# A fused gated-linear-attention and soft-mixture kernel on one core: the first head pair's gating work dealt out anew between three engines, and a fifth identity product ahead of its state product

## The chip, the cores and the metric

One core of one Trainium2 chip runs the whole program. The metric is the device time of one launch in microseconds (us), the median of several runs; lower is better. The engines named below are TensorE (PE, with its weight loads as PEld), VectorE (DVE), ScalarE (ACT), GpSimd (POOL) and SyncE (SP, which issues the DMAs). They run side by side, each through its own instructions in order, and wait for each other through semaphores.

## The reference, cut to what matters

There are 4 x 8 = 32 heads of 768 tokens with 48 channels each, all float32.

```python
f = 1.0 / (1.0 + np.exp(-f_logit))
for t in range(S):
    state = f[:, :, t, :, None] * state + np.einsum('bhd,bhe->bhde', k[:, :, t], v[:, :, t])
    y[:, :, t] = np.einsum('bhd,bhde->bhe', q[:, :, t], state)
x = y.transpose(0, 2, 1, 3).reshape(B * S, H * D)        # 3072 x 384
logits = x @ phi                                         # 32 slots, 4 for each of 8 experts
slot_input = softmax(logits, axis=0).T @ x               # dispatch
slot_out[e] = np.maximum(slot_input[e] @ w1[e], 0.0) @ w2[e]
return softmax(logits, axis=1) @ slot_out                # combine
```

## The kernel before, in words

Two heads lie together on 112 of the 128 partitions (48, a gap of 16, 48) and are called a pair. There are 16 pairs, four to a batch. The tokens of a pair are cut into 6 chunks of 128. For each pair, with the name that the plan gives each step:

- **Gates.** `e` (L325, ACT) is exp(-f), `ln` (L329, ACT) is ln(1 + that), `L` (L333, DVE) sums it along each chunk with a scan, `g` (L336) and `p` (L339, both ACT) are exp(L) and exp(-L), `dk` multiplies k by g and `dq` multiplies q by p, in place (both L342, through the helper `times`; on DVE or POOL). `pend` and `pbx` (POOL, a line of `copy`, L316, for `pbx`) take the last column of each chunk of p.
- **Products on PE.** `kt` (L362) transposes the gated k into PSUM, `kte` copies it out into `kta` (L316). `sc` (L374) makes the scores of three chunks at a time, `mask` (L379, DVE) takes them out under a triangular mask. `kv` (L408) makes each chunk's state from `kta` and v; the scan at L412 (DVE, `sb`) runs the state over the chunks. `ia` (L399) and `ie` (L422) add masked scores times v and q times state into `y`, and `ye` (ACT, L316) copies it out.
- **Mixture.** Logits (L454), transposes of y (L433), running maxima, exponentials and the slot inputs follow one and two pairs behind. After the last pair come the experts' two layers (`up` L620, `down` L666) and the combining products and stores (L712, L721).

The tail's output columns are made in two parts, columns 0 to 255 and 256 to 383 (`PARTS`, `WIDE`), and the order of its steps is written out in `ENDING`.

**What sets the order.** Each step is an `op` with a due number, an engine and the buffers that it reads and writes. A planner (`Plan.run`) holds all steps of the attention stage on a given engine in the order of their due numbers; only the DMAs on SP and the steps of the tail are placed by its estimates. Pair 0 and a few steps of pairs 1 and 2 have their due numbers in the table `START`. Pair 0's gates are done in two halves of 384 columns (called half a and half b below); all other pairs are done whole, in 768 columns. For each `gates` call a pair `es` chooses the engines: `es[0]` for `dk`, `es[1]` for `dq`, where 0 and 1 are POOL and 2 is DVE. Whether `kte` and `pbx` of pair 0 go to DVE or ACT is written at the `op`.

The step `warm` (L313) runs on PE while the first loads come in: products of the 128 x 128 identity with itself, repeated to 512 columns. Nothing reads them. Four are made before the first `kt`.

DMAs share one queue on SP and are issued in order. Weight loads (`lw1`, `lw2`) are put between the loads of q, k, f and v, and each weight load waits for a step of the computation that the planner picks, so that it isn't issued early. With three buffers for f, k and q and two for `L`, `g` and `p`, a load waits until its buffer's last reader has run.

Of the kernel before, what the change touches and what calls it, by code (L numbers as in the profile page):

```python
# [14 lines left out]
B, H, S, D = 4, 8, 768, 48  # L15
# [6 lines left out]
NP = B * H // 2  # L22
# [47 lines left out]
class Plan:  # L70
# [22 lines left out]
    def op(self, name, engs, fn, *args, r=(), w=(), x=(), due=0.0, take=(), free=(), kb=0, home=False, ni=0):  # L93

        name, mode = name if isinstance(name, tuple) else (name, None)
        deps = set()
        for key in r:
            if key in self.writer:
                deps.add(self.writer[key])
        for key in (*w, *x):  # L100
            if key in self.writer:
                deps.add(self.writer[key])
            deps.update(self.readers.get(key, ()))
        fixed = self.fixed and "SP" not in engs
# [100 lines left out]
T = 7.0  # L205
N_F, N_L, N_G, N_P, N_K, N_Q, N_V, N_SC, N_KT, N_S, N_Y = 3, 2, 2, 2, 3, 3, 4, 2, 2, 2, 3
NW1 = 7
N_WARM = 4


@with_exitstack
def gla_soft_moe_kernel(ctx: ExitStack, tc: tile.TileContext, q, k, f, v, vt, phi, w1, w2, out):
# [38 lines left out]
    pbx = [P([128, D, NM], f"pbx{i}") for i in range(N_S)]  # L251
# [19 lines left out]
    mask = P([128, C], "mask")  # L271
# [34 lines left out]
                e = 2 * qq + j  # L306
                nc.gpsimd.memset(emask[:, j, qq, 4 * e : 4 * e + 4], 1.0)

    def warm_up(o):

        u = unit(("warm",))
        for n in range(N_WARM):
            nc.tensor.matmul(u[:, :512], ident, ident.unsqueeze(1).broadcast_to([128, 4, 128]), start=True, stop=True)  # L313

    def copy(o, dst, src):
# [408 lines left out]
    op = plan.op  # L724

    def either(act, dve):
        return {"ACT": act, "DVE": dve}

    op(("warm", "square"), {"PE": 1.75 * N_WARM}, lambda o: warm_up(o), due=-50, take=[(("warm",), "a")], free=[("warm",)], ni=4 * N_WARM)
    op("consts", {"DVE": 0.5}, lambda o: consts(), w=["same"], due=30)  # L730
    op("consts_2", {"POOL": 1.0}, lambda o: consts_2(), w=["emask"], due=40)

    HALVES = (slice(0, S // 2), slice(S // 2, S))

    START = dict(
        e=(-60, -59), ln=(-58, -57), g=(-55, -52), p=(-54, -51),
        L=(-60, -59), dk=(-58, -60), dq=(-57, -55.8), mask=(-54, -53),
        kt=(-9, -7), sc=(-8, -6),
    )
    START["e", 1], START["ln", 1], START["e", 2], START["g", 1], START["p", 1], START["ln", 2] = -56, -53, -50, -49, -48, -47  # L740
    START["L", 1], START["kte", 0], START["scan", 0], START["L", 2] = -56, -55, -52, -51
    START["ye", 0], START["g", 2], START["p", 2] = -46, -45, -44
    START["pbx", 0], START["dk", 1], START["dq", 1], START["pend", 0] = -55.5, -56, -55, -54
# [4 lines left out]
    def attention(i):  # L748

        z = i * T  # L750
        F_, L_, G, PB, K, Q = (
            [(name, i % n, h) for h in range(2)]
            for name, n in (("fb", N_F), ("Lb", N_L), ("gb", N_G), ("pb", N_P), ("kb", N_K), ("qb", N_Q))
        )
        V, Y = ("vb", i % N_V), ("yT", i % N_Y)
        KT, PX, SB = ("ktb", i % N_KT), ("pbx", i % N_S), ("sb", i % N_S)
        SC = [("scb", i % N_SC, h) for h in range(2)]
        b, p = divmod(i, PPB)
# [25 lines left out]
        usual = dict(e=-2 * T - 6.9, ln=-2 * T - 5.9, L=-2 * T + 2.2, g=-2 * T + 4.4, dk=-2 * T + 3.8, p=-2 * T + 4.8, dq=-2 * T + 5.6)  # L784
        if i == 0:
            for h, cs in enumerate(HALVES):
                gates(cs, [h], {name: START[name][h] for name in usual}, NP if h else 0, (0 if h else 2, 2))
        else:
            gates(slice(0, S), [0, 1], {name: START.get((name, i), z + t) for name, t in usual.items()}, i, (0, 1))
        op("pbx", {"POOL": 0.65} if i else {"DVE": 0.4}, decay_pbx, i, r=PB, w=[PX], due=START.get(("pbx", i), z - T + 0.7))  # L790
        op("pend", {"POOL": 0.2}, decay_pend, i, r=PB, w=[("pends", i)], due=START.get(("pend", i), z - T + 1.3))
        if i == 0:
            for h in range(2):
                op(("kt", "square"), {"PE": 0.33}, kt, i, 3 * h, 3 * h + 3, r=K[h : h + 1], x=[KT], w=[KK], due=START["kt"][h], take=[] if h else [(KK, "a")], ni=6)
        else:
# [27 lines left out]
    L = B - 1  # L823
# [63 lines left out]
    n, asked = 0, set()  # L887
# [10 lines left out]
    z = NP * T + 4  # L898
# [219 lines left out]
```

## Time and profile before

| | |
|---|---|
| median of 3 runs (lowest to highest) | 175.91 us (175.73 to 176.57) |
| the profiled execution's own time | 175.81 us |
| its span, first to last instruction | 174.1 us |
| mean granted TensorE clock over the span | 0.974 |
| busy in the span: PE, DVE, ACT, POOL | 155.7, 118.1, 92.6, 90.5 us |
| HBM read, written | 48.87 MB, 4.72 MB |

Times in the profile are counted from the span's start. A row of the timeline has the start, the length, the engine, the line of the kernel, the operation, what it writes <- what it reads, the shapes, and in brackets how long the engine had been idle and what ended that. A row of the chain of waits has a start, a length and the engine and line on which the program's end hung in that stretch. A row of the windows table has a stretch, then busy time (and instructions) of PE, PEld, DVE, ACT and POOL in it, then the granted clock, the DMA engines' share and GB/s. "SPq" rows are DMAs being issued.

### The profile page before, as it was taken

The numbers are of one execution on the slowest core, as the hardware profiler recorded it, in microseconds if no ns is written. First come the engines' busy times: TensorE is split into PE (matmuls) and PEld (weight loads), VectorE is DVE, ScalarE is ACT, GpSimd is POOL, SyncE is SP. The second block draws the span as 40 slices with busy tenths as digits, with TensorE's granted clock in tenths as the row PEclk, the third lists the DMA queues.
The fourth block names the chain that finished last, engine by engine and source line by source line (L and its number), as shares of the span: only waits on it lengthen the run. The fifth ranks groups of instructions, "written<-read, shape, count | busy, mean of one in ns | idle before, by whom it ended". The sixth has DMA issues, their size and how long they took to land.

```text
span 174.1 us, 6032 instructions
## 1 busy us (share of the span) xinstructions
PE 155.7 (89%) x2546; PEld 122.5 (70%) x2546; DVE 118.1 (68%) x169; ACT 92.6 (53%) x166; POOL 90.5 (52%) x89
## 2 busy tenths in 40 slices
PE   5957999999899998999998999999899999989700
PEld 2347889988699877998986989988555454567600
DVE  2699699999998995898996989755540342143510
ACT  5880698767679677687683772542322121041500
POOL 3086298899298896997987888841000001000000
PEclk9996999999999999999999999999999999999985
DMA  5999999999999999999986659999998870029780
GB/s 145 375 407 362 351 306 332 399 395 396 397 392 397 394 395 384 391 405 390 371 281 186 168 186 293 370 395 390 397 392 315 266 284 6 2 92 402 289 315 12
DMA packets 20468, 54.08 MB, mean 311 GB/s; under 512 B 2272, under 2 KB 2640, under 8 KB 20432
## 3 DMA queue, kind: packets, MB, share of 16 engines
q1 hardware_dynamic: 20432, 53.60, 84.0%
q8 instruction: 22, 0.36, 0.8%
q14 instruction: 14, 0.11, 0.2%
HBM read 48.87 MB, written 4.72 MB: 308 GB/s over the span
## 4 chain that ended last, share of the span: by engine, by line
PE 62%; DVE 12%; POOL 11%; issue 4%; DMA 3%; ACT 2%; SPq 1%; POOLq 0%; DVEq 0%; ACTq 0%
PE y L399 9%; PE sc L374 9%; PE up L620 6%; PE y L422 5%; PE kv L408 5%; PE kt L362 5%; PE po L666 4%; PE xt L433 4%; PE pf L712 4%; POOL kb L342 3%; DMA qb<-in_q_dram 3%; POOL qb L342 3%; PE pl L454 3%; DVE Lb L333 3%; POOL ce L540 2%
## 5 line engine op out<-in xcount | busy, mean ns | idle before, releaser
L342 POOL TENSOR_TENSOR kb<-kb,gb 112x768 f32<-112x768 f32 (+1 forms) x16 | 29.7, 1854 | 24.9 <-ACT gb L336 20.5
L333 DVE TENSOR_TENSOR_SCAN Lb<-starts,fb 112x768 f32<-112x768 f32 (+1 forms) x17 | 35.0, 2064 | 2.9 <-ACT fb L329 2.9
L379 DVE TENSOR_TENSOR scb<-sc,mask 128x768 f32<-128x768 f32 x32 | 29.1, 951 | 4.2 <-PE sc L374 4.1
L342 POOL TENSOR_TENSOR qb<-qb,pb 112x768 f32<-112x768 f32 x15 | 27.5, 1832 | 0.0
L374 PE MATMUL sc<-qb,kb 48*128 48x128 f32 x384 | 26.4, 282 | 0.8 <-DVE kta L316 0.8
L399 PE MATMUL y<-scb,va 128*64 128x128 f32 (+1 forms) x384 | 26.9, 284 | 0.0
L316 ACT COPY yT<-y 112x768 f32<-112x768 f32 x16 | 12.8, 798 | 25.6 <-PE y L422 25.6
L374 PEld LDWEIGHTS sc<-qb,kb 48*128 48x128 f32 x384 | 22.9, 188 | 3.5 <-DVE kta L316 1.0
L316 POOL COPY pbx<-pb 112x240 f32<-112x240 f32 x15 | 23.6, 1575 | 0.0
L399 PEld LDWEIGHTS y<-scb,va 128*64 128x64 f32 (+1 forms) x384 | 23.1, 135 | 0.3
L540 POOL TENSOR_TENSOR ce<-ce,cm 128x256 f32<-128x256 f32 x4 | 4.7, 1166 | 29.3 <-DVE cm L537 29.3
L316 DVE COPY kta<-kt 128x672 f32<-128x672 f32 x16 | 13.5, 845 | 8.5 <-PE kt L362 8.5
L336 ACT ACTIVATE gb<-Lb 112x768 f32<-112x768 f32 (+1 forms) x17 | 13.7, 805 | 5.9 <-DVE Lb L333 5.9
L408 PE MATMUL kv<-va,kta 128*64 128x48 f32 (+1 forms) x384 | 14.7, 223 | 1.6 <-DVE kta L316 1.6
L329 ACT ACTIVATE fb<-fb,one 112x768 f32<-112x768 f32 (+1 forms) x17 | 15.1, 895 | 0.4
L408 PEld LDWEIGHTS kv<-va,kta 128*64 128x64 f32 (+1 forms) x384 | 12.7, 132 | 3.7 <-DVE kta L316 1.8
L422 PE MATMUL y<-qb,sb 48*48 48x128 f32 x320 | 14.6, 285 | 0.0
L325 ACT ACTIVATE fb<-fb 112x768 f32<-112x768 f32 (+1 forms) x17 | 13.7, 804 | 1.7 <-DMA fb<-in_f_dram 1.7
L362 PE MATMUL kt<-ident,kb 112*128 112x112 f32 x96 | 12.6, 266 | 1.5 <-POOL kb L342 1.5
L339 ACT ACTIVATE pb<-Lb 112x768 f32<-112x768 f32 (+1 forms) x17 | 13.5, 792 | 0.0
L422 PEld LDWEIGHTS y<-qb,sb 48*48 48x48 f32 x320 | 11.1, 162 | 2.9 <-DVE sb L412 2.2
L362 PEld LDWEIGHTS kt<-ident,kb 112*128 112x128 f32 x96 | 9.7, 140 | 3.4 <-POOL kb L342 1.7
(156 smaller groups left out, 260.2 us busy)
## 6 DMA issues: line engine op xcount, KB each, us to landing
w1b<-in_w_dram SPq DMA_DIRECT2D x34, 384.0 KB, 6.5
kb<-in_k_dram SPq DMA_DIRECT2D x16, 384.0 KB, 6.4
qb<-in_q_dram SPq DMA_DIRECT2D x16, 384.0 KB, 6.4
fb<-in_f_dram SPq DMA_DIRECT2D x15, 384.0 KB, 6.1
va<-in_v_dram SPq DMA_DIRECT2D x16, 288.0 KB, 6.5
out_dram<-w1b SPq DMA_DIRECT2D x6, 512.0 KB, 3.9
scb<-in_w_dram SPq DMA_DIRECT2D x4, 384.0 KB, 7.7
out_dram<-w1b SPq DMA_DIRECT2D x6, 256.0 KB, 4.3
```

What stands on the lines that cost most here:

```text
L316: {"ACT": nc.scalar.copy, "DVE": nc.vector.tensor_copy, "POOL": nc.gpsimd.tensor_copy}[o.eng](dst, src)
L325: nc.scalar.activation(t, t, AF.Exp, scale=-1.0, accum_out=esum[:, n : n + 1])
L329: nc.scalar.activation(t, t, AF.Ln, bias=one[:PW])
L333: nc.vector.tensor_tensor_scan(Lb[i % N_L][:PW, cs], flat(starts)[:PW, cs], fb[i % N_F][:PW, cs], 0.0, op0=ALU.mult, op1=ALU.add)
L336: nc.scalar.activation(gb[i % N_G][:PW, cs], Lb[i % N_L][:PW, cs], AF.Exp)
L342: (nc.vector if o.eng == "DVE" else nc.gpsimd).tensor_tensor(t, t, by, op=ALU.mult)
L362: nc.tensor.transpose(u[:, C * m : C * m + PW], kb[i % N_K][:PW, C * m : C * m + C], ident[:PW, :PW])
L374: nc.tensor.matmul(u[:, 512 * r + C * m : 512 * r + C * m + C], kb[i % N_K][rs, cs], qb[i % N_Q][rs, cs], start=True, stop=True,)
L379: nc.vector.tensor_tensor(scb[i % N_SC][:, :, h], un["sc", i, h].rearrange("p (r x) -> p r x", r=2)[:, :, : 3 * C].rearrange("p r (m t) -> ...
L399: nc.tensor.matmul(u[rows(at), y_cols(m)], va[:, v0 : v0 + (D if at else 64)], scb[i % N_SC][:, r, h, m % 3], start=m % 3 == 0, stop=False ...
L408: nc.tensor.matmul(u[rows(r), :, m], ktb[i % N_KT][:, m, rows(r)], vb[i % N_V][:, m, r], start=True, stop=True)
L422: nc.tensor.matmul(u[at : at + D, y_cols(m)], sb[i % N_S][rs, :, m - 1], qb[i % N_Q][rs, C * m : C * m + C], start=False, stop=m in (2, 5) ...
```

## The change

Its name has two parts. The part on the tail (parts of 256 and 128 columns) is in both versions word for word: `PARTS`, `WIDE`, `ENDING` and all lines of the tail are the same. What differs is the start:

```diff
-N_WARM = 4
-    def warm_up(o):
-        u = unit(("warm",))
-        for n in range(N_WARM):
+    def warm_up(o, n):
+        u = unit(o.takes[0][0])
+        for _ in range(n):
             nc.tensor.matmul(u[:, :512], ident, ident.unsqueeze(1).broadcast_to([128, 4, 128]), start=True, stop=True)
...
-    op(("warm", "square"), {"PE": 1.75 * N_WARM}, lambda o: warm_up(o), due=-50, take=[(("warm",), "a")], ...)
+    def warm(due, n, us=0.9):
+        op(("warm", "square"), {"PE": us * n}, warm_up, n, due=due, take=[(("warm", due), "b")], ...)
+    warm(-100, 4, 1.6)
...
-                gates(cs, [h], {...}, NP if h else 0, (0 if h else 2, 2))
+                gates(cs, [h], {...}, NP if h else 0, (2, 1 if h else 2))
-            gates(slice(0, S), [0, 1], {...}, i, (0, 1))
+            gates(slice(0, S), [0, 1], {...}, i, (0, 2 if i == 1 else 1))
-        op("pbx", {"POOL": 0.65} if i else {"DVE": 0.4}, decay_pbx, ...)
+        op("pbx", {"POOL": 0.65} if i else {"ACT": 0.4}, decay_pbx, ...)
-        op("kte", {"DVE": 0.86}, kt_copy, ...)
+        op("kte", {"DVE": 0.86} if i else {"ACT": 0.86}, kt_copy, ...)
...
+        if i == 0:
+            warm(-94, 1)
         op(("kv", "cols"), {"PE": 0.71}, kv, i, ...)
```

So `dk` of pair 0's half b goes from POOL to DVE, `dq` of that half from DVE to POOL, `dq` of pair 1 from POOL to DVE, and `kte` and `pbx` of pair 0 from DVE to ACT. One more identity product stands on PE between pair 0's last scores and its `kv`. The four at the start are kept, in a PSUM buffer of the other kind. The numbers in `START` are written anew to fit. In the changed file a line that was L333 is L332, and so on.

VectorE at the start of the program, before (pair 0 is `kb0`, `qb0`, `Lb0` at first; pair 1 is `kb1`, `qb1`, `fb1`; pair 2's scan reads `fb2`):

```order
L342 TENSOR_TENSOR kb0_73<-kb0_73,gb0_69 112x384
L342 TENSOR_TENSOR qb0_76<-qb0_76,pb0_71 112x384
L333 SCALAR_TENSOR_TENSOR Lb1_66<-starts_67,fb1_63 112x768
L342 TENSOR_TENSOR qb0_76<-qb0_76,pb0_71 112x384
L316 COPY pbx0_83<-pb0_71 112x48x5
L316 COPY kta_82<-kt_170 128x672
L379 TENSOR_TENSOR scb0_80<-sc_176,mask_113 128x2x384
L379 TENSOR_TENSOR scb0_80<-sc_192,mask_113 128x2x384
L412 SCALAR_TENSOR_TENSOR sb0_85<-kv_205,pbx0_83 112x288
L333 SCALAR_TENSOR_TENSOR Lb0_65<-starts_67,fb2_64 112x768
L316 COPY kta_82<-kt_250 128x672
```

VectorE at the same place in the changed program:

```order
L341 TENSOR_TENSOR kb0_73<-kb0_73,gb0_69 112x384
L341 TENSOR_TENSOR qb0_76<-qb0_76,pb0_71 112x384
L341 TENSOR_TENSOR kb0_73<-kb0_73,gb0_69 112x384
L332 SCALAR_TENSOR_TENSOR Lb1_66<-starts_67,fb1_63 112x768
L378 TENSOR_TENSOR scb0_80<-sc_172,mask_113 128x2x384
L378 TENSOR_TENSOR scb0_80<-sc_191,mask_113 128x2x384
L411 SCALAR_TENSOR_TENSOR sb0_85<-kv_207,pbx0_83 112x288
L341 TENSOR_TENSOR qb1_77<-qb1_77,pb1_72 112x768
L332 SCALAR_TENSOR_TENSOR Lb0_65<-starts_67,fb2_64 112x768
L315 COPY kta_82<-kt_254 128x672
```

Half b's `dk` now stands ahead of pair 1's scan; half b's `dq`, `pbx` and `kte` are gone from DVE, and pair 1's `dq` stands between pair 0's state scan and pair 2's gate scan.

ScalarE after pair 0's gates, before (`gb1` and `pb1` are pair 1's g and p, `yT0` is pair 0's `ye`):

```order
L325 ACTIVATE fb2_64,esum_68<-fb2_64 112x768
L336 ACTIVATE gb1_70<-Lb1_66 112x768
L339 ACTIVATE pb1_72<-Lb1_66 112x768
L329 ACTIVATE fb2_64<-fb2_64,one_122 112x768
L316 COPY yT0_87<-y_221 112x768
L336 ACTIVATE gb0_69<-Lb0_65 112x768
```

and in the changed program:

```order
L324 ACTIVATE fb2_64,esum_68<-fb2_64 112x768
L315 COPY kta_82<-kt_167 128x672
L315 COPY pbx0_83<-pb0_71 112x48x5
L335 ACTIVATE gb1_70<-Lb1_66 112x768
L338 ACTIVATE pb1_72<-Lb1_66 112x768
L328 ACTIVATE fb2_64<-fb2_64,one_122 112x768
L315 COPY yT0_87<-y_222 112x768
L335 ACTIVATE gb0_69<-Lb0_65 112x768
```

Pair 0's `kte` and `pbx` stand on ACT ahead of pair 1's g. GpSimd, from its first gate product on, before:

```order
L342 TENSOR_TENSOR kb0_73<-kb0_73,gb0_69 112x384
L342 TENSOR_TENSOR kb1_74<-kb1_74,gb1_70 112x768
L342 TENSOR_TENSOR qb1_77<-qb1_77,pb1_72 112x768
L354 COPY pends_99<-pb0_71 112x6
L316 COPY pbx1_84<-pb1_72 112x48x5
```

and in the changed program:

```order
L341 TENSOR_TENSOR qb0_76<-qb0_76,pb0_71 112x384
L341 TENSOR_TENSOR kb1_74<-kb1_74,gb1_70 112x768
L353 COPY pends_99<-pb0_71 112x6
L315 COPY pbx1_84<-pb1_72 112x48x5
L353 COPY pends_99<-pb1_72 112x6
```

Pair 1's `dq` has left POOL, and half b's `dk` there has become its `dq`. From pair 2 on the four computing engines have the same instructions in the same order in both programs, the tail among them. On SP some weight loads stand one to three places earlier or later among the loads of q, k, f and v, up to about pair 12; pair 4's f stands behind pair 2's v and not ahead of it.

More of the change, by code (lines that the diff above doesn't have):

```diff
@@ L727, in either @@
         return {"ACT": act, "DVE": dve}
-    op(("warm", "square"), {"PE": 1.75 * N_WARM}, lambda o: warm_up(o), due=-50, take=[(("warm",), "a")], free=[("warm",)], ni=4 * N_WARM)
+    def warm(due, n, us=0.9):
+        op(("warm", "square"), {"PE": us * n}, warm_up, n, due=due, take=[(("warm", due), "b")], free=[("warm", due)], ni=4 * n)
+    warm(-100, 4, 1.6)
     op("consts", {"DVE": 0.5}, lambda o: consts(), w=["same"], due=30)
@@ L735, in gla_soft_moe_kernel @@
     START = dict(
-        e=(-60, -59), ln=(-58, -57), g=(-55, -52), p=(-54, -51),
-        L=(-60, -59), dk=(-58, -60), dq=(-57, -55.8), mask=(-54, -53),
-        kt=(-9, -7), sc=(-8, -6),
-    )
[L740 to L743, printed above, removed]
+        e=(-99, -98), ln=(-97, -96), g=(-94, -91), p=(-93, -90),
+        L=(-99, -98), dk=(-97, -95), dq=(-96, -99), mask=(-93, -92),
+        kt=(-99, -96), sc=(-98, -95),
+    )
+    for n, (name, i) in enumerate(
+        [("e", 1), ("ln", 1), ("e", 2), ("kte", 0), ("pbx", 0), ("g", 1), ("p", 1), ("ln", 2), ("ye", 0), ("g", 2), ("p", 2)]
+        + [("L", 1), ("scan", 0), ("dq", 1), ("L", 2)]
+        + [("dk", 1), ("pend", 0)]
+    ):
+        START[name, i] = -80 + n
+    START["e", 1], START["ln", 1], START["L", 1] = -95, -92, -94
     def load_half(o, dst, src, cs):
@@ L786, in attention @@
             for h, cs in enumerate(HALVES):
-                gates(cs, [h], {name: START[name][h] for name in usual}, NP if h else 0, (0 if h else 2, 2))
+                gates(cs, [h], {name: START[name][h] for name in usual}, NP if h else 0, (2, 1 if h else 2))
         else:
-            gates(slice(0, S), [0, 1], {name: START.get((name, i), z + t) for name, t in usual.items()}, i, (0, 1))
-        op("pbx", {"POOL": 0.65} if i else {"DVE": 0.4}, decay_pbx, i, r=PB, w=[PX], due=START.get(("pbx", i), z - T + 0.7))
+            gates(slice(0, S), [0, 1], {name: START.get((name, i), z + t) for name, t in usual.items()}, i, (0, 2 if i == 1 else 1))
+        op("pbx", {"POOL": 0.65} if i else {"ACT": 0.4}, decay_pbx, i, r=PB, w=[PX], due=START.get(("pbx", i), z - T + 0.7))
         op("pend", {"POOL": 0.2}, decay_pend, i, r=PB, w=[("pends", i)], due=START.get(("pend", i), z - T + 1.3))
@@ L796, in attention @@
             op(("kt", "square"), {"PE": 0.65}, kt, i, r=K, x=[KT], w=[KK], due=z - T + 3.9, take=[(KK, "a")], ni=12)
-        op("kte", {"DVE": 0.86}, kt_copy, i, r=[KK], w=[KT], due=START.get(("kte", i), z - T + 4.6), free=[KK])
+        op("kte", {"DVE": 0.86} if i else {"ACT": 0.86}, kt_copy, i, r=[KK], w=[KT], due=START.get(("kte", i), z - T + 4.6), free=[KK])
         for h, key in enumerate((S0, S1)):
```

## The prediction

> **What bounds the kernel now.** I read the page first, then the chain of waits, then the windows over the start, then the timeline of each engine there. The chain, from pair 1's gate scan to pair 0's first state products:
>
> ```profile
> 8.62 1.75 DVE Lb L333
> 10.37 1.21 DVE qb L342
> 11.58 1.91 DVE pbx L316
> 13.49 0.78 DVE kta L316
> 14.31 1.22 PE kv L408 x20
> ```
>
> Nearly 6 us pass on DVE before PE gets its first `kv`, and what follows on PE is slow too. The windows (PE busy first, then PEld, DVE, ACT, POOL; then the granted clock) say why:
>
> ```profile
> 11.20:14.70 3.50, 1.83 (x30) 1.46 (x30) 3.50 (x4) 1.61 (x3) 3.37 (x2) 1.00 1.03 404
> 14.70:18.10 3.40, 3.40 (x45) 3.07 (x41) 3.40 (x4) 0.00 (x0) 1.27 (x4) 0.50 1.05 351
> ```
>
> PE stands idle for half of 11.2 to 14.7, and for the 3.4 us after that it has half its clock: pair 0's 24 `y` products took 2.85 us, pair 1's last 23 took 1.49.
>
> ```profile
> 15.27 2.85 PE L399 MATMUL y<-scb,va 128*48 128x128 f32 x24
> 21.89 1.49 PE L399 MATMUL y<-scb,va 128*64 128x128 f32 x23
> ```
>
> Why DVE is late shows in its rows beside POOL's:
>
> ```profile
> 9.05 2.12 POOL L342 TENSOR_TENSOR kb<-kb,gb 112x384 f32<-112x384 f32 x1 [6.81 <-ACT gb L336]
> 10.29 1.29 DVE L342 TENSOR_TENSOR qb<-qb,pb 112x384 f32<-112x384 f32 x1
> 11.33 1.92 POOL L342 TENSOR_TENSOR kb<-kb,gb 112x768 f32<-112x768 f32 x1 [0.16 <-ACT gb L336]
> 15.26 0.58 POOL L316 COPY pbx<-pb 112x240 f32<-112x240 f32 x1
> 22.42 1.82 POOL L342 TENSOR_TENSOR qb<-qb,pb 112x768 f32<-112x768 f32 x1
> 23.11 2.75 DVE L333 TENSOR_TENSOR_SCAN Lb<-starts,fb 112x768 f32<-112x768 f32 x1
> ```
>
> These take turns. POOL's `dk`, ready at 9.05, ends 0.80 after the scan that ended at 10.37; DVE's `dq`, begun at 10.29, ends 0.41 after POOL's end at 11.17; DVE's `pbx` (11.58 in the chain) ends at 13.49, 0.24 after POOL's end at 13.25; the scan begun at 23.11 ends 1.62 after 24.24. POOL's own `pbx`, undisturbed, takes 0.58. So a gate product, a gate scan or an SBUF copy on one of the two waits for the other's to end, and whoever waits goes next. Masks, `kte` and state scans, which read PSUM, don't wait.
>
> What sets the pace after the start is POOL's `dk`:
>
> ```profile
> 20.63 1.83 POOL L342 TENSOR_TENSOR kb<-kb,gb 112x768 f32<-112x768 f32 x1 [4.66 <-ACT gb L336]
> 39.37 1.83 POOL L342 TENSOR_TENSOR kb<-kb,gb 112x768 f32<-112x768 f32 x1 [0.50 <-ACT gb L336]
> 35.69 2.66 DVE L333 TENSOR_TENSOR_SCAN Lb<-starts,fb 112x768 f32<-112x768 f32 x1
> 41.16 1.82 POOL L342 TENSOR_TENSOR qb<-qb,pb 112x768 f32<-112x768 f32 x1
> 41.99 2.10 DVE L299 COPY same<-ident 32x128 f32<-32x128 f32 x4
> ```
>
> Three rounds of scan, g, `dk`, `dq` and again scan last 18.74 us, 6.25 each, and `dk` begins 1.02 after the scan ends (38.35 to 39.37). At 42.98 POOL's `dq` lets DVE's copies of `same` go, and the chain then runs over DVE, POOL and ACT up to 66 us. So the end moves by as much as pair 2's `dk` (20.63) does, if nothing absolute stands later.
>
> **The change, part by part.** I follow the path to that `dk`. Needed besides:
>
> ```profile
> 7.28 0.56 DVE L342 TENSOR_TENSOR kb<-kb,gb 112x384 f32<-112x384 f32 x1 [0.59 <-ACT gb L336]
> 8.40 0.51 ACT L336 ACTIVATE gb<-Lb 112x384 f32<-112x384 f32 x1
> 8.81 0.51 ACT L339 ACTIVATE pb<-Lb 112x384 f32<-112x384 f32 x1
> 11.22 0.51 PE L362 MATMUL kt<-ident,kb 112*128 112x112 f32 x3 [1.49 <-POOL kb L342]
> 10.41 0.84 ACT L336 ACTIVATE gb<-Lb 112x768 f32<-112x768 f32 x1 [0.26 <-DVE Lb L333]
> 11.72 0.94 PE L374 MATMUL sc<-qb,kb 48*128 48x128 f32 x12
> 14.18 1.81 DVE L379 TENSOR_TENSOR scb<-sc,mask 128x768 f32<-128x768 f32 x2
> 15.12 0.18 POOL L354 COPY pends<-pb 112x6 f32<-112x6 f32 x1
> 15.90 0.74 DVE L412 TENSOR_TENSOR_SCAN sb<-kv,pbx 112x288 f32<-112x288 f32 x1
> 16.57 1.73 DVE L333 TENSOR_TENSOR_SCAN Lb<-starts,fb 112x768 f32<-112x768 f32 x1
> ```
>
> DVE's rows overlap by 0.07 (15.90 + 0.74 against 16.57), so a step of DVE begins that much before the last one's end.
>
> 1. Half b's `dk` on DVE: g ends at 8.91, 0.56 more makes 9.50 (before: 11.17).
> 2. Half b's `dq` on POOL: p ends at 9.32; POOL began 0.08 after pair 1's g (11.25 to 11.33), so it is ready at 9.40 and waits for DVE till 9.50. With 0.80: 10.30.
> 3. Pair 1's scan, behind the added `dk` on DVE, would begin at 9.42 or 9.43 and finds POOL ahead of it by 0.02 us. I take that order, which is nearly a tie (first rival). It gets its turn at 10.30 and ends at 11.92, 1.55 later than before.
> 4. g to 12.80, pair 1's `dk` on POOL 12.88 to 14.71.
> 5. DVE: masks from 11.84, state scan to 14.31; then pair 1's `dq`, which must wait for POOL till 14.71. Its 768 columns on DVE aren't in the trace: twice 0.41 or twice 0.56, 0.82 to 1.12; since it has waited, 0.82: 15.53.
> 6. `pend` on POOL has waited and goes next, at most 0.18, I take 0.12: 15.65. Pair 2's scan, queued behind `dq` on DVE, takes 1.62: 17.27 (before: 18.30).
> 7. Before, pair 2's g could not begin at 18.30: it stands behind `ye` on ACT, which waited for PE.
>
> ```profile
> 19.01 0.80 ACT L316 COPY yT<-y 112x768 f32<-112x768 f32 x1 [6.20 <-PE y L422]
> 19.70 0.85 ACT L336 ACTIVATE gb<-Lb 112x768 f32<-112x768 f32 x1
> ```
>
> Now PE must be done well before 16.4. Half b's `kt` (0.51) follows its `dk` and ends at 10.2; its `sc` needs the `dq` at 10.30, then 0.94 and some 0.1 to start: 11.4. Then the added product:
>
> ```profile
> 1.95 6.63 PE L313 MATMUL warm<-ident 128*128 128x512 f32 x8 [1.95 <-POOL valid L291]
> ```
>
> The four at the start took 1.66 each; at the clock doubled, as `y` shows it, 0.83. I take 0.9: 12.3. ACT copies `kte` meanwhile: 672 columns from PSUM, not in the trace, between 0.62 (`xb`, 576) and 0.80 (`yT`, 768), so 0.7, from 10.25 to 10.95.
>
> ```profile
> 27.38 0.62 ACT L316 COPY xb<-xt 128x576 f32<-128x576 f32 x1
> ```
>
> Its `pbx`, 240 columns, costs less than the 0.51 that ACT takes for 384; I take 0.4: 11.35. Queued behind both is pair 1's g, which waits for 11.92 anyway: that 0.6 us is their cover; were it gone, both would be paid. So `kv` runs 12.3 to 13.1, `y` follows the masks (12.8 and 13.65) to 14.4, the state products follow the state scan to 15.3, `ye` is out at 16.1. The product costs nothing, since the mask at 12.8 is waited for beside it; its other PSUM buffer adds no wait, as what comes next in it is on PE too.
>
> So pair 2's g begins when its scan is done, and `dk` at 17.27 + 1.02 = 18.29, against 20.63: **2.34 us earlier**. PE's side comes along: pair 1's `kte` follows the scan at 17.2, masks to 19.9, state scan 20.6, state products at 20.75 against 23.31 (below), 2.56 earlier, so it doesn't hold the loop back.
>
> ```profile
> 23.31 0.91 PE L422 MATMUL y<-qb,sb 48*48 48x128 f32 x20
> ```
>
> The part on the tail's columns is in both versions; it is worth nothing. On SP, pair 4's f stands behind pair 2's v and waits for pair 1's scan, now 11.92; by the longest landing it is there at 19.4. Its `e` ran at 22.98 and may come 2.3 earlier, 20.7: covered. The other loads' slack, at a tight place: pair 5's q was issued at 30.64, is there by 38.1, and is read at 41.16, so 3.0 us stay, more than 2.34.
>
> ```profile
> 22.98 0.83 ACT L325 ACTIVATE fb<-fb 112x768 f32<-112x768 f32 x1
> 30.64 0.33 SPq L320 DMA_DIRECT2D qb<-in_q_dram  x1
> DMA to landing us min/median/max: 4.2/6.5/7.5
> ```
>
> The sum: the profiled execution took 175.81 (span 174.1 and 1.7 around it); 175.81 - 2.34 = 173.47. The median is 0.10 above that execution: **173.6 us**. The unknown costs (up to 0.30 more in step 5; 0.12 less to 0.06 more in step 6) and 0.1 either way for rows that overlap give 173.3 to 174.1 for this case alone.
>
> **The rivals.**
>
> *DVE goes first at 9.50.* A tie by 0.02 us can fall either way. Then the scan ends at 11.13, half b's `dq` at 11.93, its scores at 13.0; now the added product is on the path, `kv` ends at 14.7, the state scan at 15.45, pair 1's `dq` at 16.3, pair 2's scan at 17.95, `dk` at 18.97. The gain is 1.66: 174.25. The same comes if POOL's `pbx` slips ahead of pair 2's scan (0.58).
>
> *Half clock again.* The clock fell when PE was busy for 1.83 of 3.5 us. From 9.6 to 15.3 PE would now pause for well under 1 us, so I hold this unlikely. If 3.4 us at half clock begin at 11.3, the product takes 1.7 and `kv` 1.6, the state scan ends at 15.45: 174.3 again. The Trainium skill ("TensorE: Matmul & The Clock Gate", section "Why this matters for your kernels") asks only for no idle gap over about 3 us between bursts. By that rule the gaps here were harmless and one more product cures nothing; the trace disagrees, with half clock though no gap was longer than this one:
>
> ```profile
> 14.31 1.22 PE L408 MATMUL kv<-va,kta 128*64 128x48 f32 x24 [1.65 <-DVE kta L316]
> ```
>
> *Given back.* The DMA engines are full in the first 20 of 40 slices:
>
> ```profile
> DMA  5999999999999999999986659999998870029780
> ```
>
> Loads then can't all come 2.3 us sooner. If the pairs come to wait for them until the queue empties at 87 us, some 2 of the 2.34 us go again: 175.5. Against it: the 3.0 us of slack, and that many loads in the queue are weights that no product reads before the last pair is done.
>
> *Slower.* In the loop DVE's scan is ready before POOL's `dq` ends, by 1.13 us for pair 3 (23.11 against 24.24), so it beats `pbx`. If the new timing makes it come after, `pbx` goes first and each round lengthens by its 0.58. From five rounds on (2.9) the kernel is slower; seven lose 4.06 against 2.34 won: 177.6. Against it: by my sum the margin grows, state scan at 20.6 against `dq`'s end at 21.9.
>
> **How the numbers follow.** Forecast 0.50; DVE first 0.25; half clock 0.08; given back 0.10; slower 0.07. The first three (0.83) are faster by over 0.5% (0.88 us, about what a measurement can tell from no change), the fourth is the same (0.10), the last slower (0.07). Likeliest: 173.6. The range starts at the first case's 173.3, less 0.2 should the loop come to follow PE's larger lead (2.56), less 0.2 for the spread of runs (the lowest of before is 0.18 under its median): 172.9. It ends above the second and third with the same unknown costs (174.9), in the better half of the fourth: 175.2.
>
> **What would show it.** Right: granted clock 1.00 from 9 to 25; half b's `dq` on POOL ending near 10.3 and before pair 1's scan; `ye` of pair 0 near 15.3; pair 2's `dk` near 18.3; the same lead at the copies of `same` (41.99) and at the tail's first `up` product. Wrong: pair 2's `dk` later than 19.5, a clock of 0.50 before 25, ACT waiting for f from a DMA after 20 us, or a lead over before that shrinks between pair 2 and the tail.

## The result and the profile after

The changed kernel took 174.06 us, the median of 4 executions (173.58 to 174.96), against 175.97 of the kernel before (4 executions, 175.73 to 176.57): ratio 0.9893, 95% interval 0.9845 to 0.9940. That is 0.46 above the forecast and inside its range. The time came near; the way to it was not the forecast's. In the chain of waits of the changed kernel, from GpSimd's only gate product in pair 0 to pair 2's gate scan (start, duration, what):

```profile
9.47 2.51 POOL qb L341
12.03 0.94 PE sc L373 x12
12.96 1.05 PE warm L312 x2
14.02 0.86 PE kv L407 x20
15.63 0.93 DVE qb L341
16.56 1.68 DVE Lb L332
```

DVE's long run of before (8.62 to 14.31) is gone, but half b's `dq` on POOL lasts to 11.97, its scores begin only then, and the added product, which the forecast had hidden, is on the path. The rows around 9.4 us, from the timelines of ACT, DVE and POOL, and those of pair 0's `ye`, pair 2's g and pair 2's `dk`:

```profile
8.82 0.51 ACT L338 ACTIVATE pb<-Lb 112x384 f32<-112x384 f32 x1
8.95 0.56 DVE L341 TENSOR_TENSOR kb<-kb,gb 112x384 f32<-112x384 f32 x1 [0.32 <-ACT gb L335]
9.42 1.75 DVE L332 TENSOR_TENSOR_SCAN Lb<-starts,fb 112x768 f32<-112x768 f32 x1
9.47 2.50 POOL L341 TENSOR_TENSOR qb<-qb,pb 112x384 f32<-112x384 f32 x1 [7.23 <-ACT pb L338]
17.06 0.80 ACT L315 COPY yT<-y 112x768 f32<-112x768 f32 x1 [3.38 <-PE y L421]
18.27 0.84 ACT L335 ACTIVATE gb<-Lb 112x768 f32<-112x768 f32 x1 [0.40 <-DVE Lb L332]
19.19 1.84 POOL L341 TENSOR_TENSOR kb<-kb,gb 112x768 f32<-112x768 f32 x1 [4.35 <-ACT gb L335]
```

DVE's scan was there 0.05 ahead of POOL at the point where the two take turns (called the port below), kept its undisturbed 1.75, and POOL ended 0.80 after it. Pair 2's `dk` came at 19.19, 1.44 earlier than before (20.63), where the forecast had 18.29. Pair 2's gate scan ended at 18.24 in the chain, where it ended at 18.30 before: the new order won next to nothing on DVE. What moved is `ye`, from 19.01 to 17.06, so that pair 2's g no longer stands behind it on ACT. The windows over the stretch that had half the clock before (PE, PEld, DVE, ACT, POOL; then the granted clock):

```profile
11.20:14.61 3.41, 2.58 (x38) 1.71 (x40) 1.78 (x2) 2.48 (x4) 3.17 (x4) 1.00 1.04 399
14.61:18.03 3.42, 3.42 (x64) 2.96 (x61) 3.07 (x3) 0.80 (x1) 0.23 (x2) 1.00 1.04 372
```

In this execution PE kept its whole clock, and 23 of pair 0's `y` products took 1.49, where 24 took 2.85 before. The lead then stayed what it was, 1.44 at the copies of `same` (41.99 before) and 1.43 at the tail's first `up` (the first two rows are of the changed kernel, the last of before):

```profile
40.55 1.60 DVE L298 COPY same<-ident 32x128 f32<-32x128 f32 x2
127.61 1.92 PE L619 MATMUL up<-w1b,si 128*32 128x512 f32 x16
```

```profile
129.04 1.50 PE L620 MATMUL up<-w1b,si 128*32 128x512 f32 x12
```

The profiled execution took 174.06 (span 171.9), 1.75 under before's 175.81; 1.43 of it was there at the first `up`, 0.32 came after it. The span alone shrank by 2.2, which is more than was won: the time around it, which the forecast kept at 1.7, is 2.2 in the changed kernel.

Further executions showed that both kernels spread by 3 to 4 us from one execution to the next, so a single profile of each isn't a comparison. The experiments' ratios (to the kernel before on the same chip, with the 95% interval in brackets) leave out executions over 1.5% above their kernel's fastest, and beside them I give counts and medians over all. These are the profiled ones, with pair 0's first `dk` (half a, which waits for k's landing or for g, whichever comes later), pair 2's `dk`, the first `up`, the time, and half clock before 160 us:

| kernel | first dk | pair 2's dk | first up | time, us | half clock |
|---|---|---|---|---|---|
| before | 7.28 | 20.63 | 129.04 | 175.81 | 14.7 to 18.1 |
| before, again | 7.71 | 18.91 | 127.38 | 174.00 | none |
| before, third | 9.08 | 21.71 | 130.20 | 176.65 | 12.8 to 19.6 |
| changed | 7.30 | 19.19 | 127.61 | 174.06 | none |
| changed, again | 7.40 | 19.31 | 127.71 | 174.17 | none |
| changed, third | 7.54 | 20.57 | 128.95 | 175.57 | 13.6 to 17.0 |
| before, fifth product alone | 7.67 | 19.05 | 127.51 | 174.04 | none |
| before, both pauses filled | 8.54 | 19.30 | 127.75 | 174.33 | none |
| changed, pause filled | 7.56 | 19.45 | 127.88 | 174.60 | none |
| changed, no fifth product | 7.49 | 19.35 | 127.74 | 174.17 | 12.2 to 15.7 |
| changed, POOL first | 7.80 | 18.52 | 126.93 | 173.50 | none |
| changed, pair 1's dq on POOL | 8.52 | 19.76 | 129.22 | 175.78 | 20.0 to 23.4 |
| changed, half b on DVE | 7.26 | 17.89 | 126.32 | 172.49 | none |
| the same, no fifth product | 7.77 | 18.41 | 126.81 | 173.14 | none |

From the first `up` to the end of the execution (its time less the first `up`) all take 46.2 to 46.8: what tells the executions apart happens in the first 25 us.

### The profile page after: what moved, and what is told of

Same layout as the page of the kernel before. It is cut to its first block, busy times and chain, and to the rows that moved or that the text cites. A ratio compares the mean times of both kernels' runs of the same rounds, so it can differ in the third digit from the quotient of the medians.

```text
span 171.9 us, 6033 instructions
## 1 busy us (share of the span) xinstructions
PE 155.5 (90%) x2548; PEld 121.3 (71%) x2548; DVE 115.8 (67%) x168; ACT 93.8 (55%) x168; POOL 88.9 (52%) x88
## 4 chain that ended last, share of the span: by engine, by line
PE 59%; POOL 13%; DVE 10%; ACT 6%; issue 4%; DMA 2%; SPq 0%; POOLq 0%; DVEq 0%; ACTq 0%
PE sc L373 9%; PE y L398 8%; PE up L619 6%; PE kv L407 5%; PE y L421 5%; POOL qb L341 5%; PE po L665 5%; DVE Lb L332 4%; PE kt L361 4%; PE pf L711 4%; PE xt L432 4%; POOL kb L341 3%; PE pl L453 3%; DMA fb<-in_f_dram 2%; POOL ce L539 2%
## 5 line engine op out<-in xcount | busy, mean ns | idle before, releaser
L332 DVE TENSOR_TENSOR_SCAN Lb<-starts,fb 112x768 f32<-112x768 f32 (+1 forms) x17 | 35.1, 2068 | 3.2 <-ACT fb L328 3.2
L341 POOL TENSOR_TENSOR kb<-kb,gb 112x768 f32<-112x768 f32 x15 | 27.5, 1830 | 17.8 <-ACT gb L335 13.9
L341 POOL TENSOR_TENSOR qb<-qb,pb 112x768 f32<-112x768 f32 (+1 forms) x15 | 28.1, 1871 | 7.2 <-ACT pb L338 7.2
L398 PE MATMUL y<-scb,va 128*48 128x128 f32 (+1 forms) x384 | 25.8, 275 | 0.0
L315 ACT COPY yT<-y 112x768 f32<-112x768 f32 x16 | 12.8, 798 | 22.9 <-PE y L421 22.9
L398 PEld LDWEIGHTS y<-scb,va 128*64 128x64 f32 (+1 forms) x384 | 21.9, 130 | 0.6 <-DVE scb L378 0.2
L315 DVE COPY kta<-kt 128x672 f32<-128x672 f32 x15 | 12.7, 844 | 7.1 <-PE kt L361 7.1
L411 DVE TENSOR_TENSOR_SCAN sb<-kv,pbx 112x288 f32<-112x288 f32 x16 | 12.0, 749 | 1.0 <-PE kv L407 1.0
```

The lines of the kernel that those rows point to most:

```text
L315: {"ACT": nc.scalar.copy, "DVE": nc.vector.tensor_copy, "POOL": nc.gpsimd.tensor_copy}[o.eng](dst, src)
L332: nc.vector.tensor_tensor_scan(Lb[i % N_L][:PW, cs], flat(starts)[:PW, cs], fb[i % N_F][:PW, cs], 0.0, op0=ALU.mult, op1=ALU.add)
L341: (nc.vector if o.eng == "DVE" else nc.gpsimd).tensor_tensor(t, t, by, op=ALU.mult)
L398: nc.tensor.matmul(u[rows(at), y_cols(m)], va[:, v0 : v0 + (D if at else 64)], scb[i % N_SC][:, r, h, m % 3], start=m % 3 == 0, stop=False ...
```

## The experiments

The theory after the result: the changed kernel lost 0.9 of the forecast's 2.34 us because DVE's scan went ahead of POOL's `dq`, which put the scores and the fifth product on the path; and what it won was largely the clock. Rivals: the fifth product is what won, the sharing is what won, or the first comparison was luck.

**Without the fifth product.** In the changed kernel:

```
-        if i == 0:
-            warm(-94, 1)
```

> The changed kernel without the fifth identity product. In the changed kernel's trace pair 0's state scan waited for kv, and kv for that product (12.89 to 14.0), so by the theory that the product is on the path and buys nothing here, kv begins near 13.0, the state scan near 13.9, pair 1's dq waits for POOL's pbx till 14.7, pair 2's gate scan ends near 17.2 and pair 2's dk begins near 18.15, 1.0 us sooner than in the changed kernel (19.19); the time is some 1.0 us lower, 173.0. The clock stays whole, because PE's pauses are still shorter than before. By the rival, that the product holds the clock, the granted clock falls to 0.50 for 3.4 us somewhere between 11 and 21 us, y takes about 2.8 us in place of 1.5, and pair 2's dk begins no sooner than 19.2.

The median of 10 executions was 173.95 (172.41 to 174.53), ratio 0.9937 (0.9883 to 0.9992); before had 175.52, median of 25, on the same chip. Its windows and its `kv`:

```profile
8.83:12.24 3.41, 1.56 (x17) 1.23 (x19) 3.22 (x4) 3.22 (x7) 2.50 (x1) 1.00 1.03 397
12.24:15.66 3.42, 3.42 (x46) 3.20 (x46) 1.50 (x2) 1.74 (x3) 2.61 (x4) 0.50 1.04 372
```

```profile
13.50 1.30 PE L407 MATMUL kv<-va,kta 128*64 128x48 f32 x22
```

This profile had the half clock, against the theory: `kv` took 1.30 for its first 22 products, against 0.84 for 23 in the changed kernel, and pair 2's `dk` came at 19.35, only 0.16 later than with product and whole clock. So in these two profiles the product costs about what the half clock costs. The half clock and the `dk` after 19.2 are signs of the rival, but the changed kernel's third profile (below) has the half clock with the product in place, so the product doesn't keep it away. No execution of the ten was above 174.53, and their median is 1.57 under that of before: the product is not what won.

**The fifth product alone.** In the kernel before, one product between half b's scores and `kv`:

```
+    def warm_one(o):          # one such product
...
+        if i == 0:
+            op(("warm2", "square"), {"PE": 0.9}, lambda o: warm_one(o), due=-5,
+               take=[(("warm2",), "b")], free=[("warm2",)], ni=4)
```

> The kernel before with nothing but the one added identity product between pair 0's second scores and its kv. If the product keeps the clock whole: no half clock before 160 us, pair 0's kv in 0.85 and its y in about 1.5 us, its state products near 16.8 (18.05 before), its ye near 17.7, pair 2's gate scan still ending at 18.3, so pair 2's dk near 19.35 in place of 20.63, and a time 1.3 us under before, 174.6. The product itself hides, since kv waits for kta till 14.3 anyway. If the clock does not follow from PE's pauses (the rule that only gaps over 3 us matter), the half-clock stretch stays, pair 2's dk stays at 20.6 and the time at 175.9.

The median of 10 was 175.83 (174.04 to 177.20), ratio 1.0068 (1.0012 to 1.0123): the product alone wins nothing in the median. Yet the profiled execution took 174.04, with whole clock:

```profile
13.25 1.12 PE L317 MATMUL warm<-ident 128*128 128x512 f32 x2
19.05 1.83 POOL L346 TENSOR_TENSOR kb<-kb,gb 112x768 f32<-112x768 f32 x1 [0.42 <-ACT gb L340]
```

The product took 1.12, where the forecast took 0.9. In this execution POOL's `dk` of half b was also ahead of DVE's scan (8.71 against 10.04), so it differs from the first profile of before by more than the product. One profile and its own kernel's median disagreed by 1.8 us here, which is why the later runs have repeats.

**POOL first.** In the changed kernel a small memset of an unused tile holds DVE's scan back:

```
+    gap = P([128, 96], "gap")
+    op("gap", {"DVE": 0.15}, lambda o: nc.vector.memset(gap, 0.0), due=-94.5)
```

> The changed kernel with one memset of 128x96 in an unused tile on DVE between half b's dk and pair 1's gate scan, so that this scan asks for its turn about 0.1 us later (9.52 in place of 9.42, POOL asked at 9.47). If whoever asks first goes first, POOL's dq of half b runs from 9.51 to 10.3, the scan ends near 11.9, half b's scores are done near 11.4, pair 2's dk begins near 18.3 (19.19 in the changed kernel), and the time is 0.9 us under the changed kernel's, 173.2. If DVE keeps its turn from one instruction to the next, POOL's dq still ends near 12.0, the scan is merely 0.1 later, and pair 2's dk begins at 19.2 to 19.3.

```profile
9.68 1.01 POOL L341 TENSOR_TENSOR qb<-qb,pb 112x384 f32<-112x384 f32 x1 [7.44 <-ACT pb L338]
9.80 2.50 DVE L332 TENSOR_TENSOR_SCAN Lb<-starts,fb 112x768 f32<-112x768 f32 x1
18.52 1.83 POOL L341 TENSOR_TENSOR kb<-kb,gb 112x768 f32<-112x768 f32 x1 [0.43 <-ACT gb L335]
```

With the order turned, POOL's `dq` takes 1.01 and DVE's scan 2.50: the mirror image of the rows above. Pair 2's `dk` is 0.67 earlier than in the changed kernel, though k landed 0.5 later. So the order in step 3 is what the forecast lost. The median is 174.52 of only 4 executions (172.87 to 176.06): whether the order held in each of them isn't known, and the price in the median stays open.

**Pair 1's `dq` back on POOL.**

```
+    START["dq", 1] = -64.5
-            ... (0, 2 if i == 1 else 1))
+            ... (0, 1))
```

> The changed kernel with pair 1's dq back on POOL, behind pair 1's dk, as before. In the changed kernel's trace this dq stood on DVE between pair 0's state scan (to 15.72) and pair 2's gate scan (from 16.48), so by the theory that it lengthens that path, it now runs on POOL from 14.0 to 15.8 beside the masks and the state scan, pair 2's gate scan ends near 17.4 in place of 18.23, pair 2's dk begins near 18.4 (19.19), and the time is 0.8 us lower. By the rival, that moving it off POOL is what frees the loop, pair 2's dk comes later than 19.2 and the time rises.

The median of 10 was 175.19 (172.87 to 175.89), ratio 1.0005 (0.9950 to 1.0059). The theory had 0.8 less than the changed kernel; it failed, and the rival's signs came.

```profile
15.73 3.26 POOL L341 TENSOR_TENSOR qb<-qb,pb 112x768 f32<-112x768 f32 x1
```

```profile
19.04 1.27 PE L373 MATMUL sc<-qb,kb 48*128 48x128 f32 x16 [1.54 <-POOL qb L341]
```

```profile
16.54:19.95 3.41, 1.87 (x30) 1.51 (x26) 1.70 (x2) 2.34 (x4) 3.41 (x5) 1.00 1.04 383
19.95:23.37 3.42, 3.42 (x49) 3.20 (x47) 2.55 (x3) 3.35 (x7) 3.42 (x3) 0.50 1.04 400
```

On POOL the product waits for pair 2's scan (3.26 against 0.93 on DVE), PE waits 1.54 for it, and a window with 1.87 of work is followed by half clock, in pair 1 this time. By the ratios the move of pair 1's `dq` to DVE seems worth something, but this run doesn't show how much: in its profile k also landed late (first `dk` at 8.52, not 7.30), POOL's `dq` of half b was ahead (9.80), and the clock differs.

**The kernel before, again.** Unaltered, as is the changed kernel below.

> The kernel before once more, unaltered. Theory (the 3.4 us windows on which the granted clock is set fall at another time in each execution): in this profile the half clock begins at another time than 14.7 us or is missing; if it is missing, pair 2's dk comes near 19.2 to 19.6 instead of 20.63, since pair 0's products then take half the time. Rival (the half clock follows from the kernel's own pauses of PE and comes wherever they are): half clock for 3.4 us from 14 to 16 us again and pair 2's dk at 20.4 to 20.9. The median is that of before, within 0.5 us, by both.

The median of 12 was 175.49 (174.00 to 176.65). The ratio of this unaltered program to itself came out as 1.0059 (1.0013 to 1.0105), which excludes 1: the intervals here are too narrow, and ratios within about 0.6% of 1 tell nothing by themselves. Its profile, POOL and DVE at the port, pair 0's `y`, pair 2's `dk`:

```profile
8.99 1.11 POOL L342 TENSOR_TENSOR kb<-kb,gb 112x384 f32<-112x384 f32 x1 [6.74 <-ACT gb L336]
9.15 2.56 DVE L333 TENSOR_TENSOR_SCAN Lb<-starts,fb 112x768 f32<-112x768 f32 x1
14.29 1.64 PE L399 MATMUL y<-scb,va 128*48 128x128 f32 x24
18.91 1.83 POOL L342 TENSOR_TENSOR kb<-kb,gb 112x768 f32<-112x768 f32 x1 [0.36 <-ACT gb L336]
```

k and q landed a little later (first `dk` at 7.71, not 7.28), so DVE's scan came to the port at 9.15 and not at 8.62, and POOL's `dk` was first. No window fell to half clock, `y` took 1.64 and not 2.85, and pair 2's `dk` came at 18.91: 0.28 earlier than in the changed kernel. That is earlier still than the 19.2 to 19.6 which the theory gave for whole clock. The profile on which the forecast rests had two things against it that this one had not: the order at the port and the half clock.

**The changed kernel, again.**

> The changed kernel once more, unaltered, on the chip of the other runs of this call. Theory (the gain is the 1.44 us by which pair 2's dk came earlier, and the clock's 3.4 us windows fall otherwise in each execution): a median 1.2 to 1.9 us under that of before, a spread of 1.5 us or more between the fastest and the slowest execution, DVE's pair-1 scan ahead of POOL's half-b dq, and pair 2's dk between 18.9 and 19.8 us. Rival (the difference of the first comparison was mostly luck of the windows): a median within 0.9 us of that of before. If POOL goes first this time, the order of the two is itself settled anew in each execution and pair 2's dk comes near 18.5.

The median of 6 was 174.83 (172.69 to 176.23) against 175.41 of 17; ratio 0.9884 (0.9803 to 0.9964). DVE was first again (9.55 against 9.57), pair 2's `dk` at 19.31. The spread that the theory expected is there; over all executions the medians are only 0.58 apart, as the rival had it.

**Half b wholly on DVE.** Half b's `dq` too, ahead of pair 1's scan, so that nothing is left to decide:

```
-        ... dq=(-96, -99), ...
+        ... dq=(-96, -94.5), ...
-                gates(cs, [h], ..., NP if h else 0, (2, 1 if h else 2))
+                gates(cs, [h], ..., NP if h else 0, (2, 2))
```

> The changed kernel with half b's dq on DVE too, ahead of pair 1's scan, so that POOL has none of half b's gate products and nothing is left to decide between the two. Theory (the lost 0.9 us came from POOL's dq waiting for the scan and from the scores, the fifth product and kv behind it): half b's dq ends near 9.9 us, pair 1's scan near 11.6, kv begins by 12.7, the state scan by 13.8, pair 2's dk comes at 17.9 to 18.3, 0.9 to 1.3 earlier than in the changed kernel's profile, and the median is 0.5 to 1.3 us under that of the changed kernel in this call. Rival (pair 2's dk is held by something else, the port between pair 1's dk and dq or the loads): pair 2's dk at 18.9 or later and the median within 0.4 us of the changed kernel's.

The median of 6 was 172.48 (171.93 to 173.57), ratio 0.9855 (0.9801 to 0.9909), the best of all: 2.35 under the changed kernel's median on the same chip.

```profile
9.39 0.55 DVE L341 TENSOR_TENSOR qb<-qb,pb 112x384 f32<-112x384 f32 x1
9.86 1.75 DVE L332 TENSOR_TENSOR_SCAN Lb<-starts,fb 112x768 f32<-112x768 f32 x1
17.89 1.83 POOL L341 TENSOR_TENSOR kb<-kb,gb 112x768 f32<-112x768 f32 x1 [0.42 <-ACT gb L335]
```

```profile
10.08 0.94 PE L373 MATMUL sc<-qb,kb 48*128 48x128 f32 x12
12.00 0.84 PE L407 MATMUL kv<-va,kta 128*64 128x48 f32 x23
```

The `dq` delays the scan by 0.44, the scores come 1.95 earlier, `kv` too, and pair 2's `dk` 1.30 earlier, at the early edge of what was expected. The median moved by more than that. The mean granted clock of each execution, which the section on the prediction uses below, splits the 2.35 roughly: the changed kernel's four executions on this chip with 0.978 or more had a median of 173.81, 1.33 above this one. The rest goes with the half clock, for which its other two executions have the low mean (0.963 and 0.970) and none of these six clearly does (0.975 or more). PE has no pause over 0.62 us left in the start of this profile.

**The same without the fifth product.**

> The same as the run with half b's dq on DVE, without the fifth identity product. Theory (with the scores done at 11 us the fifth product is covered, since kv then still ends before the second mask): state scan and pair 2's dk within 0.2 us of the run with it if no window has half the clock, up to 1.5 later if one begins between 11 and 15 us; median within 0.4 us of the run with it. Rival (the fifth product is on the path there too): pair 2's dk 0.6 to 0.9 earlier and the median 0.5 or more lower.

The median of 6 was 172.71 (171.82 to 173.56), ratio 0.9862 (0.9809 to 0.9915).

```profile
13.74 0.75 DVE L411 TENSOR_TENSOR_SCAN sb<-kv,pbx 112x288 f32<-112x288 f32 x1
18.41 1.84 POOL L341 TENSOR_TENSOR kb<-kb,gb 112x768 f32<-112x768 f32 x1 [0.43 <-ACT gb L335]
```

The first `dk` was 0.51 later in this execution (7.77 against 7.26), the state scan 0.50 (13.24 with the product), pair 2's `dk` 0.52. So with the scores done by 11 us the product is covered, as step 7 of the prediction supposed; it wins nothing there either.

**The changed kernel with its pause filled.** A sixth product, between half a's and half b's scores:

```
+            if i == 0 and h:
+                warm(-95.5, 1)
```

> The changed kernel with a sixth identity product, between the first half's scores and the second half's scores, where PE waits nearly 2 us for half b's dq; nothing reads it. From the profiles so far: a window of 3.41 us in which PE was busy for 1.87 us or less was followed by half clock, one with 1.93 or more was not. In the changed kernel's profile a window that began anywhere from about 8.3 to 10.4 us would have held 1.9 us of work or less, in some 6 of 10 executions, as windows begin at any time; with the product the least window holds some 2.35. Theory (the wide spread of the changed kernel's executions is half clock in some of them): no half clock before 160 us, no execution above 175.2, the median 0.3 to 1.0 us under that of the changed kernel in this call. Rival (the spread has another source, the landing of the first loads or the program's end): executions above 175.5 remain, median within 0.3 us.

The median of 12 was 174.06 (173.75 to 174.74), ratio 0.9950 (0.9919 to 0.9982).

```profile
10.72:14.13 3.41, 2.33 (x16) 1.04 (x14) 2.43 (x3) 3.17 (x5) 3.23 (x2) 1.00 1.03 406
14.13:17.55 3.42, 3.42 (x72) 3.02 (x72) 2.43 (x4) 0.22 (x1) 0.92 (x4) 1.00 1.05 364
```

The spread fell from 3.97 us (the third set of the changed kernel, same chip, 173.04 to 177.01) to 0.99, and nothing above 175.2 is left, as the theory had it: most of the spread hung on PE's pause. The lowest times went too (five executions of the changed kernel were under 173.75, the lowest 172.69); why, no run shows.

**The kernel before with both pauses filled.**

```
+    def warm_one(o):          # one such product
...
+        if i == 0:
+            for due in (-7.5, -5):
+                op(("warm2", "square"), {"PE": 0.9}, warm_one, due=due,
+                   take=[(("warm2", due), "b")], free=[("warm2", due)], ni=4)
```

> The kernel before with two identity products more, one in each of the two pauses of PE in its first pair, ahead of half b's kt and ahead of kv; nothing reads them. Theory (most of what the change won is the clock): no half clock before 160 us, the median 0.9 to 1.8 us under that of before and within 0.6 us of the changed kernel with its sixth product. Rival (the new sharing of the work wins by itself, 1.4 us or more): the median stays 1.2 us or more above that of the changed kernel with its sixth product.

The median of 12 was 174.28 (173.98 to 176.07, one above 175.2), ratio 0.9972 (0.9935 to 1.0009), against 175.24 of 35 of before on the same chip.

```profile
6.76:10.18 3.42, 1.77 (x6) 0.49 (x4) 1.22 (x2) 2.23 (x5) 1.24 (x1) 1.00 1.00 358
10.18:13.59 3.41, 3.17 (x30) 2.26 (x30) 3.41 (x6) 2.46 (x5) 0.59 (x1) 1.00 1.04 412
```

Two products that nothing reads win 0.96 in the median, and with the pauses filled in both the two kernels are 0.22 apart: the new sharing by itself, in the order in which it comes out, is worth little. The first window is one with 1.77 of work and no half clock behind it, which the rule in the expectation of the last run below did not allow.

**The changed kernel, a third time.**

> The changed kernel unaltered, a third profile and more times. Theory: DVE's scan of pair 1 ahead of POOL's half-b dq again unless the first k and q land later than 7.3 and 8.1 us by 0.4 or more; if the window that begins between 8.3 and 10.4 us holds 1.9 us of PE's work or less, half clock follows it and pair 2's dk comes later than 19.5 us. Rival: no half clock in this kernel whatever the windows. Median 1.0 to 1.8 us under that of before.

The median of 12 was 174.70 (173.04 to 177.01), ratio 0.9939 (0.9893 to 0.9985); over all executions it is 0.54 under that of before, not 1.0 to 1.8. DVE was first once more (9.67 against 9.71), and this time the half clock came, behind a window with 1.57 of work as the theory had it:

```profile
10.20:13.61 3.41, 1.57 (x16) 1.06 (x15) 2.42 (x3) 3.34 (x7) 3.12 (x2) 1.00 1.03 405
13.61:17.02 3.41, 3.41 (x37) 2.31 (x37) 1.29 (x3) 0.37 (x1) 1.50 (x4) 0.50 1.06 362
```

```profile
13.14 1.64 PE L312 MATMUL warm<-ident 128*128 128x512 f32 x2
14.71 1.30 PE L407 MATMUL kv<-va,kta 128*64 128x48 f32 x22
```

The fifth product took 1.64 and not 1.12, `kv` 1.30 and not 0.84; pair 2's `dk` came at 20.57, as late as before, in a kernel that was to cure that.

**The kernel before, a third time.**

> The kernel before unaltered, a third profile. Theory: where k lands so late that half b's first dk on POOL begins ahead of pair 1's scan (some 0.4 us later than in the first profile) pair 2's dk comes near 18.9, as in the second profile, otherwise near 19.2 to 19.6 with whole clock and 20.4 to 20.9 with half clock between 13 and 19 us; half clock follows exactly those windows in which PE was busy for 1.9 us of 3.41 or less. Rival: half clock without such a window, or such a window without half clock behind it.

The median of 12 was 175.96 (173.69 to 176.84), ratio 1.0011 (0.9961 to 1.0061). k landed late (first `dk` at 9.08), and POOL's `dk` started before pair 1's scan (10.83), but pair 2's `dk` did not come near 18.9:

```profile
5.97:9.38 3.41, 1.66 (x4) 0.38 (x2) 1.05 (x2) 3.31 (x7) 0.22 (x1) 1.00 1.00 361
9.38:12.79 3.41, 1.88 (x18) 1.34 (x18) 2.99 (x4) 1.11 (x3) 1.11 (x1) 1.00 1.04 410
12.79:16.21 3.42, 3.04 (x39) 2.84 (x41) 3.08 (x5) 2.23 (x3) 2.68 (x2) 0.50 1.01 366
16.21:19.62 3.41, 3.41 (x41) 3.07 (x40) 2.42 (x2) 0.00 (x0) 3.17 (x4) 0.50 0.92 301
```

Two windows in a row had half clock, and pair 2's `dk` came at 21.71. The expectation left the clock out of its first case, and its rule fell: the window at 5.97, with 1.66 of work, was not followed by half clock.

## Why the prediction was right in its number, and where it failed

**Step 1** held: half b's `dk` ended at 9.51 (9.50 forecast).

**Steps 2 and 3 failed.** "Finds POOL ahead of it by 0.02 us" rested on POOL starting 0.08 after ACT's end; it started 0.14 after (8.82 + 0.51 = 9.33, 9.47). The 0.08 was read off pair 1's `dk`, for which POOL had been idle for 0.16 us. The nearer row was half b's own `dk`, after 6.81 us of idling: g ended at 8.40 + 0.51 = 8.91 and POOL began at 9.05, 0.14 later. With that the forecast would have had POOL at 9.46, behind DVE. DVE's scan came at 9.42, as forecast, and won. It won by 0.02 to 0.05 in all three profiles of the changed kernel, and the run with POOL first shows what the order is worth: pair 2's `dk` at 18.52, near the forecast's 18.29.

**The end of step 6 failed with them, the core of step 7 held.** The forecast took 1.03 of its gain from the end of pair 2's gate scan (17.27 in place of 18.30) and most of the rest from g, which was no longer to wait behind `ye`. The scan ended at 18.24, so the first part was nearly nothing; g began at 18.27, right behind the scan, with `ye` out of its way, and that is nearly all of the 1.44. `ye` came 1.95 earlier (though at 17.06 and not near 15.3), most of it from `y` at whole clock (1.49 for 23 products against 2.85 for 24). So in these two profiles the gain comes from the clock more than from the new sharing.

**"The product costs nothing" failed with step 3.** It held where the scores were done at 11 us (half b on DVE); here they end at 12.96.

**The first rival came instead**, step by step: scan to 11.17 (11.13 by its working), `dq` to 11.97 (11.93), scores to 12.96 (13.0), `kv` to 14.88 (14.7), pair 2's `dk` at 19.19 (18.97). Its gain of 1.66 became 1.44; the term mis-sized is the product, 1.12 instead of 0.9. 175.81 - 1.44 = 174.37; the rest to 174.06 came after the first `up`.

**Half clock again, at 0.08, was priced too low.** Its ground, that PE "would pause for well under 1 us", fell with step 3: PE waits 1.90 before half b's scores. It came in one of three profiles of the changed kernel. How often it comes can be read from the mean granted clock, which is on record for each execution outside the first set of before (the half clock after PE's last product is in every mean). The five profiles with half clock before 160 us had a mean of 0.974 or less, the nine without it 0.978 or more. By this measure, over all chips:

| | executions | 0.978 or more: median | 0.974 or less: median | between |
|---|---|---|---|---|
| before | 100 | 12: 173.94 us | 78: 175.71 us | 10 |
| changed | 22 | 12: 173.90 us | 10: 175.72 us | none |

One execution of before (185.67) is left aside. At like clock the two kernels have nearly the same medians. By this measure the change won because the half clock comes less often (10 of 22 executions, against at least 78 of 100); the medians over all are 174.31 and 175.5. The filled pauses say the same (0.22 left between the two kernels). That the mean stands for the half clock in an execution without a profile, and that nothing else differs between the two groups, is not shown.

**The number was helped by luck.** All four executions of the changed kernel in the first comparison had 0.979 or more, which is 12 of 22 over all; the first comparison's difference of 1.91 is 1.2 over all executions. The later medians of the changed kernel, 174.83 and 174.70, are still inside the range, but 1.1 to 1.2 above the forecast and not 0.46.

**The base was a gap too.** The sum took one execution of before as what the change would meet: scan ahead of `dk` and half clock. Another execution of the same program had neither, and pair 2's `dk` at 18.91, ahead of the changed kernel's 19.19. The three first runs of before lay within 0.84 us and did not give that away.

**Given back** and **Slower** didn't come: the lead at pair 2 is the lead at the first `up` (1.44 and 1.43), and the later rounds keep their 6.25 (pair 5's `dk` at 37.88 less pair 4's at 31.63).

## What to carry to other kernels

Where two engines take turns at a port and arrive within 0.1 us of each other, don't forecast the order: price both, or give one engine both pieces, as the best version here does. Where a profile shows half clock behind a pause of PE, look for the pause in the changed order too, wherever the windows may fall, and take a second profile of the kernel before as the base. Compare executions at like granted clock before crediting a change with a gain. A spread of 4 us over executions is itself a finding: filling one pause with a product that nothing reads cut it to 1 us.

## What the runs showed of the hardware

- The granted clock is set on windows of 3.41 us that begin at another time in each execution (the first whole-clock window between 5.2 and 7.9 us). The Trainium skill ("TensorE: Matmul & The Clock Gate", Part 1) calls the window free-running, and the traces agree.
- In the first 25 us, from the second whole-clock window on, windows with 1.56, 1.57, 1.76, 1.87 and 1.88 us of PE's work were followed by half clock, those with 2.25 or more were not. At the end of the program windows with 2.02 to 2.26 were followed by it too, so PE's busy time isn't the whole measure. The first whole-clock window was never followed by it, in 14 profiles, even with 1.66 and 1.77: why is open.
- No pause of PE between that first window's start and 25 us was longer than 2.07 us. The Trainium skill ("TensorE: Matmul & The Clock Gate", section "Why this matters for your kernels") warns of idle gaps over about 3 us; here half clock came without one, and the measurements decide.
- Half clock once lasted two windows (12.8 to 19.6), the first of them with 3.04 us of work, at the end of a pause of 0.83 (12.34 to 13.17); in the other four cases the half-clock window was full (3.41) and the next one had the whole clock.
- Half a's `dk` began between 7.26 and 9.08 us, as the first loads landed: it waits for k, and for g, which stands on ACT behind pair 1's f. The order at the port moved with it. In the kernel before DVE's scan went first where half a's `dk` came at 7.28, and POOL's `dk` where it came at 7.71 and 9.08. With the changed kernel's half b DVE was first in five profiles (first `dk` at 7.30 to 7.56), and POOL in the one of the run with pair 1's `dq` on POOL (8.52).
